# A condition vector fetched through the GpSimd queue, and the first two projections copied whole

## The chip, the cores and the metric

The kernel runs on one core of one Trainium2 chip. A core has five engines that run their own instruction streams side by side: TensorE (PE, matmuls and transposes into PSUM), ScalarE (ACT), VectorE (DVE), GpSimd (POOL) and SyncE (SP, which here only issues DMAs). They meet at semaphores. DMAs are issued by SP, and a few by ACT; sixteen DMA engines carry them out. The metric is the time of one execution in microseconds on the device, as the median over runs.

## The reference

A transformer block with adaptive layer norm, on one sequence of 2048 rows of 512 values (bf16):

```
mod = (silu(c) @ w_mod).reshape(1, 6, 1, 512)      # sa, ca, ga, sb, cb, gb
h = layernorm(x) * (1 + ca) + sa
q = (h @ wq)                                        # 32 heads of 128
k, v = last 512 rows of the caches                  # 8 groups, 4 heads each
o = softmax(q @ k.T / sqrt(128)) @ v
x = x + ga * (o @ wo)
h = layernorm(x) * (1 + cb) + sb
x = x + gb * (relu(h @ w1) @ w2)                    # inner width 1792
```

c is one row of 512 values; w_mod is 512 x 3072.

## The kernel before, in words

The rows are cut into 4 blocks of 512 (QB), and each block into 4 tiles of 128 rows. A unit is one block and one head: 128 units. For a unit, PE makes the projection of the head (4 matmuls of 512 columns, transposed so that the head's 128 values lie on the partitions), the scores against 512 keys (4 matmuls of 512 columns, in two pairs), and the product with the values (16 matmuls of 129 columns). ACT copies each projection from PSUM into a tile qT (L1485) and takes the exponential of each pair of scores (L1493); DVE divides by the row sums (L1503, L1504). The projection of a unit is made two units ahead (QA = 2), so the projections of units 0 and 1 are made before the main loop (L1689) starts. Output projections and, at the end, the two MLP layers fill PE as well.

A small scheduler, KB, keeps one list of operations for each engine in program order. Each operation names the resources that it reads and writes (`R_...`), and the scheduler turns them into semaphore waits. So the order of the Python lines is the order on each engine, and an operation that waits holds up everything behind it on its engine. `dma(..., eng=...)` puts a DMA into the stream of the engine named, SP if none is.

The change lies in the part before the main loop. That part goes as follows.

- Loads (L1559 to L1567). SP issues the first half of block 0's x, then c (as 4 rows of 128, into c_row), then the first half of the weights for the first two modulation vectors (`load_wm01(0)`, rows 0 to 255 of w_mod), then wq for heads 2 and 3, k and v of group 0. ACT issues the other half of x, the other half of those modulation weights, and wq for heads 0 and 1.
- POOL (L1568 to L1576) fills constants: ones, the exponent -0.5, the identity (affine select), epsilon, -1, the ones column beside v, and the constants added to the modulation columns.
- PE (L1578 to L1580) runs 7 warm-up matmuls on ones, transposes c (`silu_exp`, L1416), and runs 9 more warm-ups. ACT takes exp(-c) and a copy of c from PSUM, POOL makes silu from them (`silu_mul`, L1421 to L1423).
- Layer norm of block 0: DVE takes the statistics of tiles 0 to 2 (L1382, L1383), ACT those of tile 3 (L1582 to L1585), POOL raises to the power -0.5 (L1591), DVE normalises tiles 0 to 2 (L1393), POOL tile 3 (L1604).
- PE transposes tile 0 (L1375), makes the eight modulation columns of the first two vectors with 32 matmuls of one column each into bank 4 (`mod_cols_mm`; row chunks 0 and 1 of w_mod come from the first half of the weights, 2 and 3 from the second), and transposes tiles 1 to 3. DVE adds the constants (L1438).
- The transposed tiles get scale and shift in halves of 256 columns, on DVE (L1630) and ACT (L1632). `TB` names the banks in which the transposes stand: one row for each half, one entry for each chunk of 128 values.
- Then the projections of units 0 and 1 in halves of 256 columns. The first half of unit 0 goes to bank 4 (QBK), that of unit 1 to bank 5, the second half of unit 0 to bank 6, that of unit 1 to bank 4. ACT copies the two first halves (L1613), DVE the two second halves (L1611). A resource R_q1 stands for the second halves, and the scores of units 0 and 1 wait for both (L1492).

Of the kernel before, what the change touches and what calls it, by code (L numbers as in the profile page):

```python
# [8 lines left out]
ACTF = mybir.ActivationFunctionType  # L9
# [1189 lines left out]
def build_fast(nc, es, top, A_x, A_k_cache, A_v_cache, A_wq, A_wo, B_x, B_w1, B_w2, c, w_mod, out, flag):  # L1199
    P = 128  # L1200
# [24 lines left out]
    NQT = 3  # L1225
    VW = P + 8

    def T(name, shape, dt=BF):
        return es.enter_context(nc.sbuf_tensor(name, shape, dt))
# [6 lines left out]
    kT_sb = T("kT", [P, G, W])  # L1236
# [3 lines left out]
    qT = [T(f"qT{i}", [P, QB]) for i in range(NQT)]  # L1240
# [16 lines left out]
    c_row = T("c_row", [DC, P])  # L1257
# [10 lines left out]
    pr = [gaf[:, :], prv[:, 0:D], prv[:, D:2 * D], gbf[:, :]]  # L1268
# [9 lines left out]
    s_ps = [es.enter_context(nc.psum_tensor(f"psS{i}", [P, 2, 512], F32)) for i in range(2)]  # L1278
# [3 lines left out]
    bank = [s_ps[0][:, 0, :], s_ps[0][:, 1, :], s_ps[1][:, 0, :], s_ps[1][:, 1, :], q_ps[:, :],  # L1282
            o_ps[:, 0:2, :].rearrange("p a b -> p (a b)"), o_ps[:, 2:4, :].rearrange("p a b -> p (a b)"), w_ps[:, :]]
    QBK, WBK = 4, 7

    sem = lambda name: top.enter_context(nc.semaphore(name))
    kb = KB(nc)
    PE = kb.stream("pe", sem("s_pe"))
    ACT = kb.stream("act", sem("s_act"))
    DVE = kb.stream("dve", sem("s_dve"))  # L1290
    POOL = kb.stream("pool", sem("s_pool"))
    SP = kb.stream("sp", sem("s_sp"))

    def dsem(key):
        if key not in kb.dma_cnt:
            kb.add_dma_sem(key, sem("d_" + key))
        return key

    def dma(out_ap, in_ap, key, reads=(), writes=(), transpose=False, eng=None):
        k = dsem(key)  # L1300
        if transpose:
            return kb.op(SP, lambda e: e.dma_start_transpose(out_ap, in_ap), reads=reads, writes=writes, dma_sem=k)
        return kb.op(eng or SP, lambda e: e.dma_start(out_ap, in_ap), reads=reads, writes=writes, dma_sem=k)  # L1303

    RL = lambda name, n: [Res(f"{name}{i}") for i in range(n)]
    R_x, R_wq, R_wo = RL("x", NT), RL("wq", H), RL("wo", NPASS)
    R_kT, R_v, R_v1 = RL("kT", G), RL("v", G), Res("v1")
    R_hT, R_h2T = [RL(f"hT{i}_", DC) for i in range(2)], [RL(f"h2T{i}_", DC) for i in range(2)]
    R_qT, R_PT, R_o, R_oT = RL("qT", NQT), [RL(f"PT{i}_", 2) for i in range(NPT)], RL("o", NOS), RL("oT", NOT)
# [3 lines left out]
    R_b = RL("bank", 8)  # L1313
    R_ident, R_ones, R_c, R_sc, R_scf, R_tmp, R_cst = (Res(n) for n in ("ident", "ones", "c", "sc", "scf", "tmp", "cst"))
# [1 line left out]
    R_pr = [R_ga] + RL("pr", 2) + [R_gb]  # L1316
    R_st, R_mv, R_rstd = RL("st", NT), RL("mv", NT), RL("rstd", NT)
    R_h0 = RL("h0", DC)
    R_q1 = RL("q1_", 2)
    R_cf, R_m01 = Res("cf"), Res("m01")  # L1320
    R_s3, R_eps = Res("s3"), Res("eps")
    R_rinv, R_vmax, R_chk, R_good, R_flag = Res("rinv"), Res("vmax"), Res("chk"), Res("good"), Res("flag")
# [13 lines left out]
    def load_wq(h0, n, eng=None):  # L1336
        dma(wq_sb[:, :, h0 * Dh:(h0 + n) * Dh], wqv[:, :, h0 * Dh:(h0 + n) * Dh], f"wq{h0}", writes=R_wq[h0:h0 + n], eng=eng)
# [12 lines left out]
    def load_wm01(i, eng=None):  # L1350
        c0, c1 = i * DC // 2, (i + 1) * DC // 2
        dma(wm01[:, c0:c1, :], wm01v[:, c0:c1, :], f"wm{i}", writes=[R_wm[i]], eng=eng)

    def wm_res(sl, cc):
        return R_wm[cc // (DC // 2)] if sl < 2 else R_wm[sl]
# [15 lines left out]
    def mm(out_ap, lhsT, rhs, start, stop, reads, bk, signal):  # L1371
        kb.op(PE, lambda e: e.matmul(out_ap, lhsT, rhs, start=start, stop=stop), reads=reads, group_writes=[R_b[k] for k in bk], signal=signal)  # L1372
# [32 lines left out]
    def ln_tposes(tl, bks):  # L1405
        for cc in range(DC):
            bk = bks[cc]
            o = (cc % 2) * 512 + tl * P
            tpose(bank[bk].bitcast(BF)[:, o:o + P], xn[:, tl, cc * P:(cc + 1) * P], [R_xn[tl]], [bk], cc == DC - 1)

    CC_ORDER = (0, 2, 1, 3)
    QA = 2
# [12 lines left out]
    def mod_cols_mm(which, bk):  # L1425
        fs = []
        for cc in range(DC):
            for sl in (0, 1):
                for c2 in range(DC):
                    last = sl == 1 and c2 == DC - 1 and cc == DC - 1  # L1430
                    fs.append(lambda sl=sl, c2=c2, cc=cc, col=sl * DC + c2, last=last: mm(
                        bank[bk][:, col:col + 1], wm[sl][:, cc, c2 * P:(c2 + 1) * P], sc_bf[:, cc:cc + 1],
                        cc == 0 and sl == 0 and c2 == 0, last, [R_sc, wm_res(sl, cc)], [bk], last))
        return fs
# [49 lines left out]
    def q_evac(u, bk=QBK):  # L1484
        kb.op(ACT, lambda e: e.activation(qT[u % NQT][:, :], bank[bk], ACTF.Copy), reads=[R_b[bk]], writes=[R_qT[u % NQT]])  # L1485

    def s_mms(u, pr):
        b, h = units[u]
        g = h // R
        for i in range(2):  # L1490
            kc = pr * 2 + i
            mm(s_ps[pr][:, i, :], kT_sb[:, g, kc * P:(kc + 1) * P], qT[u % NQT][:, :], True, True, [R_kT[g], R_qT[u % NQT]] + ([R_q1[u]] if u < QA else []), [kc], i == 1)  # L1492
        kb.op(ACT, lambda e: e.activation(PT[u % NPT][:, pr * 2:pr * 2 + 2, :], s_ps[pr][:, :, :], ACTF.Exp, scale=scale),  # L1493
              reads=[R_b[pr * 2], R_b[pr * 2 + 1]], writes=[R_PT[u % NPT][pr]])

# [62 lines left out]

    for i in range(2):  # L1559
        dma(x_sb[:, 2 * i:2 * i + 2, :], xv[:, 2 * i:2 * i + 2, :], f"xa{i}", writes=R_x[2 * i:2 * i + 2], eng=ACT if i else SP)  # L1560
    dma(c_row[:, :], c[0].rearrange("(c p) -> c p", p=P), "c", writes=[R_c])
    load_wm01(0)
    load_wm01(1, ACT)
    load_wq(0, 2, ACT)
# [4 lines left out]
    kb.op(POOL, lambda e: e.memset(cst[:, 0:1], -0.5), writes=[R_cst])  # L1569
    kb.op(POOL, lambda e: e.affine_select(ident[:, :], ones[:, :], pattern=[[1, P]], compare_op=ALU.is_equal, fill=0.0,  # L1570
                                          base=0, channel_multiplier=-1), reads=[R_ones], writes=[R_ident])
    kb.op(POOL, lambda e: e.memset(cst[:, 1:2], eps), writes=[R_eps])
    kb.op(POOL, lambda e: e.memset(cst[:, 3:4], -1.0), writes=[R_eps])
    kb.op(POOL, lambda e: e.memset(v_sb[:, :, :, P:VW], 1.0), writes=[R_v1])
# [15 lines left out]
    def rstd_pow(lo, hi):  # L1590
# [12 lines left out]
    ln_norm(1)  # L1603
    kb.op(POOL, lambda e: e.tensor_scalar(xn[:, t3, :], x_sb[:, t3, :], s3[:, 1:2], rstd[:, t3:t3 + 1], op0=ALU.add, op1=ALU.mult),  # L1604
          reads=[R_x[t3], R_rstd[t3], R_s3], writes=[R_xn[t3]])
    TB = [[0, 0, 2, 2], [1, 1, 3, 7]]
    def q_evac_half(u, hf, bk, eng):
        src, dst = bank[bk][:, hf * HB:(hf + 1) * HB], qT[u][:, hf * HB:(hf + 1) * HB]
        w = [R_q1[u]] if hf else [R_qT[u]]
        if eng is DVE:  # L1610
            kb.op(DVE, lambda e: e.tensor_copy(dst, src), reads=[R_b[bk]], writes=w)  # L1611
        else:
            kb.op(ACT, lambda e: e.activation(dst, src, ACTF.Copy), reads=[R_b[bk]], writes=w)  # L1613

    ln_tposes(0, TB[0])
    fs = mod_cols_mm(0, QBK)
    for f in fs:
        f()
    ln_norm(2)
    mod_cols_evac(0, QBK)  # L1620
    HB = QB // 2
    R_half = [R_h0, R_hT[0]]

    def mod_half(hf, cc, eng):
        bk = TB[hf][cc]
        o = (cc % 2) * 512 + hf * HB
        src, dst = bank[bk].bitcast(BF)[:, o:o + HB], hT[0][:, cc, hf * HB:(hf + 1) * HB]
        sc, sh = modc[:, DC + cc:DC + cc + 1], modc[:, cc:cc + 1]
        if eng is DVE:
            kb.op(DVE, lambda e: e.tensor_scalar(dst, src, sc, sh, op0=ALU.mult, op1=ALU.add), reads=[R_b[bk], R_moda], writes=[R_half[hf][cc]])  # L1630
        else:
            kb.op(ACT, lambda e: e.activation(dst, src, ACTF.Identity, bias=sh, scale=sc), reads=[R_b[bk], R_moda], writes=[R_half[hf][cc]])  # L1632

    def q_half(u, hf, order, bk):
        for cc in order:
            mm(bank[bk][:, hf * HB:(hf + 1) * HB], wq_sb[:, cc, u * Dh:(u + 1) * Dh], hT[0][:, cc, hf * HB:(hf + 1) * HB], cc == CC_ORDER[0], cc == CC_ORDER[-1],
               [R_wq[u], R_half[hf][cc]], [bk], cc == CC_ORDER[-1])

    for tl in range(1, TPB):
        ln_tposes(tl, TB[tl // 2])  # L1640
    mod_half(0, 0, DVE)
# [5 lines left out]
    mod_half(1, 2, ACT)  # L1647
    mod_half(1, 1, DVE)
    mod_half(1, 3, DVE)
    q_evac_half(0, 0, QBK, ACT)  # L1650
    q_half(1, 0, CC_ORDER, 5)
    q_evac_half(1, 0, 5, ACT)
    q_half(0, 1, CC_ORDER, 6)
    q_evac_half(0, 1, 6, DVE)
    q_half(1, 1, CC_ORDER, QBK)
    q_evac_half(1, 1, QBK, DVE)
    load_wq(R, R)
    load_k(1)
    load_v(1)
# [5 lines left out]
    for g in range(G):  # L1665
        for i, op in enumerate((ALU.max, ALU.min)):
            add((3, 5, 12, 16, 20, 24, 28, 32)[g], lambda g=g, i=i, op=op: kb.op(DVE, lambda e: e.tensor_reduce(vmax[:, i, g:g + 1], v_sb[:, g, :, 0:Dh], axis=AX.XY, op=op),
                                                             reads=[R_v[g]], writes=[R_vmax]))
# [20 lines left out]
    for s in range(NU):  # L1689
        run_tasks(s, 100)  # L1690
        if wo_ready and wo_ready[0][0] <= s:
            _, b_, j_ = wo_ready.popleft()
            enqueue_wo(b_, j_)
        s_mms(s, 0)
        if s + QA < NU:
            q_mms(s + QA)
        s_mms(s, 1)
        if s >= 1:
            pv_mms(s - 1)
        pop_bg(4)  # L1700
# [100 lines left out]
def bass_adaLN_cond__sliding_block_cached__dense_activation_relu__prompt_kernel(  # L1801
# [14 lines left out]
    with ExitStack() as top:  # L1816
        flag = top.enter_context(nc.sbuf_tensor("flag", [1, 8], mybir.dt.int32))
        with ExitStack() as es:
            kb, fast, cut, dma_cnt, flag_ev = build_fast(nc, es, top, *args, flag)
            sems = dict(kb.sems)  # L1820
            meet = top.enter_context(nc.semaphore("s_meet"))
# [71 lines left out]
```

## Time and profile before

| | us |
|---|---|
| median of 3 runs | 560.51 |
| the runs | 561.1, 560.51, 560.2 |
| profiled execution, its own time | 561.1 |
| its span | 559.4 |
| PE busy | 550.5 (98%) |
| ACT busy | 348.9 (62%) |
| DVE busy | 253.8 (45%) |
| POOL busy | 54.7 (10%) |

The span runs from the first to the last instruction of the profile; the run's own time is 1.7 us longer. A row of the profile names the kernel's line, the engine, the operation, what it writes and reads by the program's names, and how often; bank names are psS (banks 0 to 3), psQ (4), psO (5 and 6) and psW (7). Where a helper issues the instruction the line is that of the helper: L1372 is every matmul, L1303 every plain DMA. The letter q behind an engine (SPq) marks its queue of issued instructions, PEld the loading of weights into PE. The text in square brackets is the idle time before an instruction and what ended it. DMA traffic is heaviest at the start: in the first tenth of the span the engines move about 225 GB/s, over the whole span 76.

### The profile page before, as it was taken

The page shows a single profiled execution, that of the slowest core. Times are in us where ns is not written, and L with a number is a line of the kernel's source. Part 1 is how long each engine was busy: PE and PEld are TensorE (multiplying, and loading weights), DVE is VectorE, ACT ScalarE, POOL GpSimd, SP SyncE. Part 2 cuts the span into 40 slices and gives each one's busy share as a digit, 9 for nine tenths or more (in the row PEclk, how much of TensorE's full clock was granted, in tenths as well). Part 3 has the DMA queues.
Part 4 walks back from the last instruction along what each step waited for, and adds up shares of the span by engine and source line. Part 5 has one row for each costly group of instructions (what it writes and reads, how often), then busy time and mean ns, then how long its engine had stood idle before and what let it go on. Part 6 is the DMA issues. An engine that isn't in the chain of part 4 may idle for free.

```text
span 559.4 us, 9666 instructions
## 1 busy us (share of the span) xinstructions
PE 550.5 (98%) x4060; PEld 315.8 (56%) x4134; DVE 253.8 (45%) x551; ACT 348.9 (62%) x453; POOL 54.7 (10%) x53
## 2 busy tenths in 40 slices
PE   8999999999999999999999999999999999999998
PEld 4665555555555555555555555555555654444444
DVE  4455555553546544335445443333354448321134
ACT  4986666666666666666666666666666644432500
POOL 3000022004410000033000000332000000000000
DMA  9897763513114144352352412111215110210001
GB/s 268 248 207 174 143 169 46 114 39 76 40 38 76 39 73 117 58 133 57 94 95 57 76 40 39 39 39 38 39 39 76 39 30 0 44 34 23 22 29 47
DMA packets 113309, 42.67 MB, mean 76 GB/s; under 512 B 93928, under 2 KB 112104, under 8 KB 113256
## 3 DMA queue, kind: packets, MB, share of 16 engines
q1 hardware_dynamic: 112024, 40.82, 34.3%
q10 hardware_dynamic: 1232, 1.15, 0.6%
q8 instruction: 33, 0.54, 0.4%
q14 instruction: 20, 0.16, 0.1%
HBM read 18.35 MB, written 2.10 MB: 37 GB/s over the span
## 4 chain that ended last, share of the span: by engine, by line
PE 98%; issue 1%; DMA 1%; DVE 0%; SPq 0%; DVEq 0%
PE psS L1372 28%; PE psO L1372 27%; PE psQ L1372 23%; PE psW L1372 20%; DMA c_row<-in_c_dram 1%; DVE qT L1611 0%; DVE hT L1630 0%; SPq L1303 0%; DVE PT L1723 0%; DVE PT L1725 0%; PE psS L1375 0%; PE psO L1416 0%; DVE modc L1438 0%; DVEq L123 0%
## 5 line engine op out<-in xcount | busy, mean ns | idle before, releaser
L1493 ACT ACTIVATE PT<-psS 128x1024 bf16<-128x1024 f32 x256 | 262.7, 1028 | 128.2 <-PE psS L1372 128.1
L1372 PE MATMUL psS<-qT,kT 128*128 128x512 bf16 x508 | 150.9, 379 | 0.5 <-DVE qT L1611 0.4
L1372 PEld LDWEIGHTS psO<-v,PT 128*128 128x128 bf16 x2048 | 126.6, 98 | 30.2
L1372 PE MATMUL psO<-v,PT 128*128 128x129 bf16 x2048 | 137.0, 220 | 0.0
L1372 PE MATMUL psQ<-hT,wq 128*128 128x512 bf16 (+1 forms) x510 | 130.5, 377 | 0.3 <-DVE hT L1630 0.2
L1503 DVE RECIPROCAL rinv<-psO 128x4 f32<-128x4 f32 x128 | 23.3, 182 | 227.2 <-PE psO L1372 227.2
L1372 PE MATMUL psW<-wo,oT 128*128 128x512 bf16 x454 | 118.1, 379 | 3.0
L1504 DVE TENSOR_TENSOR o<-psO,rinv 128x512 bf16<-128x512 f32 x128 | 88.5, 691 | 4.9 <-DVE rinv L1503 0.5
L1372 PEld LDWEIGHTS psQ<-hT,wq 128*128 128x128 bf16 x512 | 49.9, 98 | 60.3 <-issue 0.6
L1372 PEld LDWEIGHTS psS<-qT,kT 128*128 128x128 bf16 x512 | 49.5, 98 | 58.9 <-ACT PT L1493 0.7
L1485 ACT ACTIVATE qT<-psQ 128x512 bf16<-128x512 f32 x126 | 74.7, 593 | 0.0
L1712 ACT ACTIVATE wq<-psS 128x512 bf16<-128x512 f32 x56 | 33.4, 597 | 49.3 <-PE psS L1372 48.9
L1372 PEld LDWEIGHTS psW<-wo,oT 128*128 128x128 bf16 x512 | 45.0, 98 | 32.9 <-DVE acc L1526 1.2
L1526 DVE TENSOR_TENSOR acc<-psW,acc 128x512 f32<-128x512 f32 x48 | 33.2, 691 | 6.5 <-PE psW L1372 6.5
L1372 PE MATMUL psO<-wmw,wq 128*128 128x512 bf16 (+1 forms) x165 | 32.8, 352 | 0.3
L1529 POOL TENSOR_TENSOR acc<-acc,gaf 128x512 f32<-128x512 f32 x12 | 15.6, 1303 | 146.7 <-DVE acc L1526 139.8
L1388 POOL TENSOR_TENSOR rstd<-rstd,cst 128x4 f32<-128x4 f32 x7 | 7.2, 1025 | 216.8 <-DVE rstd L1387 216.8
L1723 DVE TENSOR_TENSOR PT<-psO,gbf 128x512 f32<-128x512 f32 (+1 forms) x12 | 7.5, 624 | 40.4 <-PE psO L1372 40.4
L1372 PE MATMUL psS<-h2T,wmw 128*128 128x512 bf16 x109 | 25.0, 379 | 0.2
L1372 PEld LDWEIGHTS psO<-wmw,wq 128*128 128x128 bf16 x168 | 15.3, 98 | 16.5
L1372 PE MATMUL psS<-hT,wmw 128*128 128x512 bf16 x110 | 24.4, 379 | 0.1
L1382 DVE BATCH_NORM_STATS2 st<-x 128x6 f32<-128x512 bf16 x31 | 21.1, 681 | 4.8 <-DMA x<-in_A_x_dram 4.8
(85 smaller groups left out, 192.6 us busy)
## 6 DMA issues: line engine op xcount, KB each, us to landing
wo<-in_A_wo_dram SPq DMA_DIRECT2D x4, 1024.0 KB, 5.9
wq<-in_A_wq_dram SPq DMA_DIRECT2D x7, 512.0 KB, 4.6
wmw<-in_B_w_dram SPq DMA_DIRECT2D x14, 256.0 KB, 3.1
wmw<-in_w_mod_dram SPq DMA_DIRECT2D x5, 512.0 KB, 4.8
oT<-o SPq DMA_TRANSPOSE x128, 2.4
out_dram<-PT SPq DMA_DIRECT2D x15, 128.0 KB, 1.7
x<-in_A_x_dram SPq DMA_DIRECT2D x3, 512.0 KB, 4.3
v<-in_A_v_cache_dram SPq DMA_DIRECT2D x8, 128.0 KB, 3.8
```

Of the source, the lines that this page charges most:

```text
L1372: kb.op(PE, lambda e: e.matmul(out_ap, lhsT, rhs, start=start, stop=stop), reads=reads, group_writes=[R_b[k] for k in bk], signal=signal)
L1382: kb.op(DVE, lambda e: e.bn_stats(st[:, t, :], x_sb[:, t, :]), reads=[R_x[t]], writes=[R_st[t]])
L1388: kb.op(POOL, lambda e: e.tensor_tensor(rstd[:, sl], rstd[:, sl], cst[:, 0:1].to_broadcast([P, hi - lo]), op=ALU.pow), reads=R_rstd[sl] + ...
L1485: kb.op(ACT, lambda e: e.activation(qT[u % NQT][:, :], bank[bk], ACTF.Copy), reads=[R_b[bk]], writes=[R_qT[u % NQT]])
L1493: kb.op(ACT, lambda e: e.activation(PT[u % NPT][:, pr * 2:pr * 2 + 2, :], s_ps[pr][:, :, :], ACTF.Exp, scale=scale), reads=[R_b[pr * 2], R ...
L1503: kb.op(DVE, lambda e: e.reciprocal(rinv[:, u, :], o_ps[:, :, P]), reads=[R_b[5], R_b[6]], writes=[R_rinv])
L1504: kb.op(DVE, lambda e: e.tensor_tensor(o_sb[u % NOS][:, :, :], o_ps[:, :, 0:P], rinv[:, u, :].unsqueeze(2).to_broadcast([P, TPB, P]), op=A ...
L1526: kb.op(DVE, lambda e: e.tensor_tensor(acc[:, tl, :], bank[WBK], acc[:, tl, :], op=ALU.add), reads=[R_b[WBK], R_acc[tl]], writes=[R_acc[tl]])
L1529: kb.op(eng, lambda e: e.tensor_tensor(acc[:, tl, :], acc[:, tl, :], gaf[:, :], op=ALU.mult), reads=[R_acc[tl], R_ga], writes=[R_acc[tl]])
L1712: kb.op(ACT, lambda e: e.activation(h1T[b % 2][:, fc, :], bank[bk], ACTF.Relu), reads=[R_b[bk]], writes=[R_h1[b % 2][fc]], pre=all_events( ...
L1723: kb.op(DVE, lambda e: e.tensor_tensor(yt[i][:, c0:c1], bank[bk][:, c0:c1], gbf[:, c0:c1], op=ALU.mult), reads=[R_b[bk], R_gb], writes=[R_ ...
```

## The change

The fetch of c leaves SP's queue, where it stood second, and is issued by GpSimd behind the affine select that makes the identity. On SP the first half of the modulation weights is then second. Half of the 32 modulation column matmuls run ahead of the transposes of tile 0. The copies in halves are gone: units 0 and 1 keep one bank each (4 and 5) for both halves of the projection, and each leaves with one ACT copy of 512 columns (`q_evac`, L1485), so that R_q1 is no longer needed. The last chunk of the second half is transposed into bank 6 in place of 7.

```diff
@@ s_mms
-            mm(s_ps[pr][:, i, :], kT_sb[:, g, kc * P:(kc + 1) * P], qT[u % NQT][:, :], True, True, [R_kT[g], R_qT[u % NQT]] + ([R_q1[u]] if u < QA else []), [kc], i == 1)
+            mm(s_ps[pr][:, i, :], kT_sb[:, g, kc * P:(kc + 1) * P], qT[u % NQT][:, :], True, True, [R_kT[g], R_qT[u % NQT]], [kc], i == 1)
@@ loads
-    dma(c_row[:, :], c[0].rearrange("(c p) -> c p", p=P), "c", writes=[R_c])
     load_wm01(0)
     load_wm01(1, ACT)
...
     kb.op(POOL, lambda e: e.affine_select(ident[:, :], ones[:, :], pattern=[[1, P]], compare_op=ALU.is_equal, fill=0.0,
                                           base=0, channel_multiplier=-1), reads=[R_ones], writes=[R_ident])
+    dma(c_row[:, :], c[0].rearrange("(c p) -> c p", p=P), "c", writes=[R_c], eng=POOL)
     kb.op(POOL, lambda e: e.memset(cst[:, 1:2], eps), writes=[R_eps])
@@ transposes and modulation columns
-    TB = [[0, 0, 2, 2], [1, 1, 3, 7]]
-    def q_evac_half(u, hf, bk, eng):
...
+    TB = [[0, 0, 2, 2], [1, 1, 3, 6]]
+    fs = mod_cols_mm(0, QBK)
+    for f in fs[:len(fs) // 2]:
+        f()
     ln_tposes(0, TB[0])
-    fs = mod_cols_mm(0, QBK)
-    for f in fs:
+    for f in fs[len(fs) // 2:]:
         f()
@@ projections of units 0 and 1
-    q_evac_half(0, 0, QBK, ACT)
     q_half(1, 0, CC_ORDER, 5)
-    q_evac_half(1, 0, 5, ACT)
-    q_half(0, 1, CC_ORDER, 6)
-    q_evac_half(0, 1, 6, DVE)
-    q_half(1, 1, CC_ORDER, QBK)
-    q_evac_half(1, 1, QBK, DVE)
+    for u, bk in ((0, QBK), (1, 5)):
+        q_half(u, 1, CC_ORDER, bk)
+        q_evac(u, bk)
```

More of the change, by code (lines that the diff above doesn't have):

```diff
@@ L1318, in build_fast @@
     R_h0 = RL("h0", DC)
-    R_q1 = RL("q1_", 2)
     R_cf, R_m01 = Res("cf"), Res("m01")
@@ L1605, in build_fast @@
           reads=[R_x[t3], R_rstd[t3], R_s3], writes=[R_xn[t3]])
-    TB = [[0, 0, 2, 2], [1, 1, 3, 7]]
-    def q_evac_half(u, hf, bk, eng):
[L1608 to L1613, printed above, removed]
+    TB = [[0, 0, 2, 2], [1, 1, 3, 6]]
+    fs = mod_cols_mm(0, QBK)
+    for f in fs[:len(fs) // 2]:
+        f()
     ln_tposes(0, TB[0])
-    fs = mod_cols_mm(0, QBK)
-    for f in fs:
+    for f in fs[len(fs) // 2:]:
         f()
```

## The prediction

> **What bounds the kernel now.** I read the page first (busy shares, then the chain that ended last), then the chain in order of time for the first 18 us, then the timeline of those microseconds by engine. The page says that TensorE (PE) is busy 98% of the span and that it carries the chain:
>
> ```profile
> PE 98%; issue 1%; DMA 1%; DVE 0%; SPq 0%; DVEq 0%
> ```
>
> So a microsecond saved or lost ahead of the first score matmul moves everything behind it by about as much; after 13.6 us PE shows no idle time worth naming. The edits lie wholly ahead of that point, where the chain in order of time is not compute (columns: start us, us, what):
>
> ```profile
> 0.79 0.40 SPq L1303
> 1.19 0.06 issue
> 1.24 3.66 DMA c_row<-in_c_dram
> ...
> 4.95 0.18 PE psO L1416
> 5.13 3.86 PE psW L1372 x9
> 8.98 0.22 PE psS L1375 x4
> 9.21 0.79 PE psQ L1372 x32
> ...
> 12.55 0.44 DVE qT L1611
> 12.99 0.35 issue
> 13.34 0.38 PE psS L1372
> ```
>
> The reader should see that the fetch of c, 1 KB, sets the start of everything: it is issued at 1.24, lands at 4.90, its transpose runs, and the nine warm-up matmuls queued behind that transpose hold PE until 8.82. At the other end stand the copies of the first projections out of PSUM. From the timeline (start, us, engine, line):
>
> ```profile
> 1.32 0.29 POOL L1570 TENSOR_SCALAR_AFFINE_SELECT ident<-ones 128x128 bf16<-128x128 bf16 x1 [0.30 <-POOL cst L1569]
> 1.66 0.41 SPq L1303 DMA_DIRECT2D wmw<-in_w_mod_dram  x1
> 4.95 0.18 PE L1416 MATMUL psO<-ident,c_row 4*128 4x4 bf16 x1 [0.73 <-DMA c_row<-in_c_dram]
> 5.43 0.28 POOL L1421 TENSOR_SCALAR tmp<-tmp 128x4 f32<-128x4 f32 x1 [3.17 <-ACT c_f L1418]
> 5.80 1.04 POOL L1422 TENSOR_TENSOR tmp<-tmp,cst 128x4 f32<-128x4 f32 x1
> 7.82 1.22 DVE L1393 TENSOR_SCALAR xn<-x,mv,rstd 128x512 bf16<-128x512 bf16 x3
> 8.82 0.39 PE L1375 MATMUL psS<-ident,xn 128*128 128x128 bf16 x4
> 12.55 0.43 DVE L1611 CAST qT<-psO 128x256 bf16<-128x256 f32 x1 [0.57 <-PE psO L1372]
> ```
>
> GpSimd (POOL) is free from 2.27 to 5.43, and PE stood idle 0.73 us for c.
>
> **The change part by part.**
>
> *c moves to POOL's queue.* Its issue goes behind the affine select, which ends at 1.61; on SP it was issued at 1.24, so 0.37 is given away at once. No row shows a DMA issued by POOL, so the time from issue to landing is bounded. From below: the quickest plain transfer in the view of DMA issues, 32 KB of the output at the quiet end, takes 1.5 us from issue to landing; 1.61 + 1.5 = 3.1. From above: c keeps the 3.66 it needed on SP, and software on POOL adds one small POOL operation, for which I take the 1.04 of the power on four columns (L1422): 1.61 + 1.04 + 3.66 = 6.3. Further off lies, in the same view, the 7.3 of the wq load on ACT's queue, which stood behind two large loads: 8.9. My value is near the middle of the first two: 1.61 + 1.04 + 1.5 = 4.15 quiet, plus 0.45 for other traffic (the excess of c on SP over a quiet transfer is 3.66 - 1.5 = 2.16; I take a fifth, since on a queue of its own c no longer stands behind the 256 KB of x, which land at 4.79, a tenth of a microsecond before c). That gives 4.6, **0.3 earlier** than 4.90; the ends give 1.8 earlier and 1.4 later.
>
> A later c is passed on in full. Queued behind the transpose on PE are the nine warm-ups (3.86); behind the two ACT copies of c are the statistics of tile 3 (L1582 to L1585); on POOL the silu and, behind it, the two powers for rstd, for which DVE's L1393 and then PE's transposes wait. An earlier c is passed on until x takes over: DVE's statistics start when x lands at 4.79 and its last small step ends at 7.69, so L1393 can start no earlier than 7.70 in place of 7.82.
>
> The memsets that POOL now issues after the transfer (L1572 to L1576, to 2.27 now) end some 1.04 later, at 3.3; the first reader is POOL's own L1421 at 5.43, so 2.1 us of cover hide them.
>
> [...]
>
> *SP's queue moves up.* w_mod's first half, wq for heads 2 and 3, k and v of group 0 and every later SP load are issued 0.42 earlier (1.66 - 1.24). The first half landed 6.3 after issue, at 7.9, and was first read at 9.0: 1.1 us of cover, so on the present path this is worth nothing. wq and k land by 9.8 and are read at 13.1. It would matter only if PE got to the modulation columns before 7.9.
>
> *Half of the 32 column matmuls go ahead of tile 0's transposes.* 0.79 and 0.22 lie in a row on PE now and then; the sum is the same while the normalised tile is ready (L1393's first third ends at 8.23) before the warm-ups end. Nothing, unless c is so early that PE waits for the tile. The bank of one transposed chunk (7 to 6) changes no order.
>
> *The first two projections leave in whole copies by ACT.* Now DVE copies the second half of unit 0 in 0.43 from 12.55, and the scores' weight load starts at 13.10. After, ACT copies all 512 columns from 12.55; this row has the time:
>
> ```profile
> L1485 ACT ACTIVATE qT<-psQ 128x512 bf16<-128x512 f32 x126 | 74.7, 593 | 0.0
> ```
>
> 0.59 - 0.43 = **+0.17** on the path. The two early ACT half copies (0.38 each, 11.68 to 12.50) ran beside PE and save nothing. Unit 1's copy follows on ACT until 13.73; the first exponential, now at 13.76, would be due at 13.93, so 0.2 us hide it. Bounds: 0 (ACT starts earlier than DVE did) and 0.6 (unit 1's copy in the way).
>
> **The sum** against the profiled execution: -0.3 + 0.17 = -0.1 on its 561.1 (span 559.4 and 1.7 around it). That run lies 0.6 above the median of the three, so on the median, 560.5, I forecast **560.4 us**. Its own range: c between 4.2 and 5.8, 559.9 to 561.6.
>
> **The rivals.**
>
> *Slower: GpSimd's transfer lands late.* One mechanism: descriptors made by software behind other POOL work, or a first use with a cost of its own, in a stage where the DMA engines are full from 2 us on. For it: 0.37 is lost at the start, no row shows such a transfer, and even on SP a 1 KB transfer took 3.66. Against: POOL is idle for three microseconds there. It decides from c at about 5.8 (+0.9 + 0.17 = +1.1). At 6.3 it gives 1.4 + 0.17 = +1.6, 562.1; at 8.9 it gives 4.0 + 0.17 = +4.2, 564.7.
>
> *Faster: c is early enough to close PE's gap.* If it lands by 4.2, PE never idles and x's statistics set the pace: transposes of tile 0 at 8.16 (L1393 from 7.70, 0.41 for a tile, 0.05) in place of 8.82, then 0.22 and the second half of the columns, 0.4, to 8.8; DVE's third L1393 runs to 9.04, and modc follows at 9.06 in place of 10.02. That is -0.96 + 0.17 = -0.8, 559.7. This is where the reordered columns and the earlier w_mod pay, since the first half needs w_mod by 7.7. To pass 0.2% it must bring 0.3 more, for which the warm-ups are a source: they start 0.43 apart, while later 512-column matmuls of the projections start 0.22 apart, so PE changes rate near 8.8. Without the gap the change could come earlier.
>
> *It moves nothing:* c lands at 4.9 as before, since the DMA engines are shared, and the copies cost their 0.17: 560.7.
>
> [...]
>
> **How the numbers follow.** Of a change of this kernel, 0.2%, 1.1 us, is about what a measurement can tell; the three runs spread over 0.9. Chances: forecast 0.40; it moves nothing 0.05 (both within 0.2%); slower rival 0.38; faster rival 0.17, of which 0.14 for going past 559.4. So faster 0.14, within 0.2% 0.40 + 0.05 + 0.03 = 0.48, slower 0.38. Both signs have weight, so the range is wider than the forecast's own: below to 559.3 (the faster rival with some rate gain), above to 562.8, which takes in c at 6.3 (562.1) and a later one by 0.7, and leaves the far end out.
>
> **What would show it.** In the new trace: the DMA issue on POOL near 1.6 and the c transpose on PE (L1416 now) at about 4.65, with PE's idle time before it near 0.4 us. If that transpose stands after 5.85 the slower rival holds, before 4.25 the faster one. Tile 0's transposes should follow it by some 3.9 us plus the first 16 columns; if they come later than that, w_mod's first half was late. The first whole ACT copy should take 0.59 and the first score matmul should start about 0.1 earlier than 13.34 in all. A first exponential further than 0.45 behind that matmul would show unit 1's copy in the way. The prediction is wrong as a whole if time after 14 us changes: it assumes the rest is only shifted.

## The result, and the profile after

The changed kernel takes 564.66 us (median of 6 runs, 564.01 to 564.86) against 560.55 before (6 runs, 560.2 to 561.1): ratio 1.007, 95% interval 1.0057 to 1.0083, 4.1 us slower. It lies outside the predicted range, which ended at 562.8, and on the side of the slower rival. The profiled execution took 564.17, its span is 562.4.

The chain of the changed kernel in order of time, first 18 us (start us, us, what):

```profile
1.33 0.26 POOL ident L1568
1.59 6.41 DMA c_row<-in_c_dram
8.00 0.05 issue
8.05 0.17 PE psO L1415
8.22 3.73 PE psW L1371 x9
...
12.99 0.18 DVE modc L1437
...
15.52 0.61 ACT qT L1484
16.13 0.35 issue
16.48 0.38 PE psS L1371
```

Everything hangs on c as before, but c lands at 8.00 in place of 4.90, 6.41 us after its issue. The later stations keep their distances: from the landing of c to modc 5.12 us before, 4.99 now; from modc to the first recorded score matmul 3.32 before, 3.49 now. So 3.10 - 0.13 + 0.17 = 3.14, and the score matmul moved from 13.34 to 16.48; the span grew by 3.0. The timeline shows what waited:

```profile
1.59 0.85 POOL L1303 DMA_DIRECT2D c_row<-in_c_dram  x1
4.90 0.69 DVE L1381 BATCH_NORM_STATS2 st<-x 128x6 f32<-128x512 bf16 x1 [4.90 <-DMA x<-in_A_x_dram]
8.05 0.17 PE L1415 MATMUL psO<-ident,c_row 4*128 4x4 bf16 x1 [3.82 <-DMA c_row<-in_c_dram]
8.53 0.28 POOL L1420 TENSOR_SCALAR tmp<-tmp 128x4 f32<-128x4 f32 x1 [5.36 <-ACT c_f L1417]
10.92 1.22 DVE L1392 TENSOR_SCALAR xn<-x,mv,rstd 128x512 bf16<-128x512 bf16 x3 [3.11 <-POOL rstd L1590]
```

x landed 0.1 us later than before and DVE's statistics of it were done at 7.8, but DVE waited 3.11 us for POOL, which stood behind the silu, and PE idled 3.82. The queues of the stretch from 2.44, where POOL's instruction ends, to 5.75, and of the stretch from there to 7.5 (kind: packets, MB, share of the DMA engines):

```profile
q1 hardware_dynamic: 335, 0.64, 54.8%
q10 hardware_dynamic: 258, 0.50, 41.3%
```

```profile
q10 hardware_dynamic: 366, 0.38, 64.0%
q1 hardware_dynamic: 379, 0.24, 43.8%
q0 software_dynamic: 32, 0.00, 1.2%
```

POOL's own queue, q0, moves nothing for 3.3 us after its instruction has ended; its 32 packets then stand among those of the other two queues. Busy time by stretch (us; length, PE, PEld, DVE, ACT, POOL, with the number of instructions in brackets, granted clock, DMA share, GB/s):

```profile
4.20:8.00 3.80, 0.02 (x1) 0.00 (x0) 2.73 (x8) 0.00 (x0) 0.00 (x0) 1.00 1.05 351
8.00:10.00 2.00, 1.95 (x6) 0.79 (x7) 0.00 (x0) 1.68 (x7) 1.33 (x2) 0.57 1.31 200
```

PE is empty until c lands, and then shows a granted clock of 0.57. The nine warm-ups take about as long as in the profiled execution of before (3.73 against 3.86), so between these two that costs nothing.

The medians differ by 4.1, the two profiled executions by 3.1. The profiled execution of before was the slowest of its six runs (561.1, 0.55 over the median), the one of after lies 0.5 under its median.

### The profile page after: what moved, and what is told of

It is laid out like the page before. It is cut to its first block, busy times and chain, and to the rows that moved or that the text cites. A ratio compares the mean times of both kernels' runs of the same rounds, so it can differ in the third digit from the quotient of the medians.

```text
span 562.4 us, 9664 instructions
## 1 busy us (share of the span) xinstructions
PE 550.3 (98%) x4060; PEld 315.8 (56%) x4134; DVE 253.0 (45%) x549; ACT 349.3 (62%) x453; POOL 55.7 (10%) x54
## 4 chain that ended last, share of the span: by engine, by line
PE 97%; DMA 1%; issue 1%; DVE 0%; ACT 0%; POOL 0%; POOLq 0%; DVEq 0%
PE psS L1371 28%; PE psO L1371 26%; PE psQ L1371 23%; PE psW L1371 20%; DMA c_row<-in_c_dram 1%; ACT qT L1484 0%; DVE hT L1623 0%; DVE PT L1713 0%; DVE PT L1715 0%; POOL ident L1568 0%; PE psS L1374 0%; POOL ones L1566 0%; DVE modc L1437 0%; PE psO L1415 0%; POOL cst L1567 0%
```

## The experiments

Times are medians, beside the kernel before on the same chip (560.3 to 560.4 in these comparisons), with the ratio and its 95% interval where several executions were timed.

**c alone on POOL** (half copies, banks and column order of before)

```diff
-    dma(c_row[:, :], c[0].rearrange("(c p) -> c p", p=P), "c", writes=[R_c])
...
+    dma(c_row[:, :], c[0].rearrange("(c p) -> c p", p=P), "c", writes=[R_c], eng=POOL)
     kb.op(POOL, lambda e: e.memset(cst[:, 1:2], eps), writes=[R_eps])
```

> The kernel before with one edit: c is issued by GpSimd behind the affine select; half copies, banks and column order stay. Theory (the late landing of c is the whole loss but for 0.17): c lands between 7.5 and 8.5 and the time is 564.0 to 564.7, some 3.5 to 4.1 above before. Rival (the whole copies or the reordered columns cost what the late c does not explain): below 563.5.

564.21 (1.0067, 1.0051 to 1.0084). Its chain:

```profile
1.59 6.54 DMA c_row<-in_c_dram
```

c landed at 8.1. This one line carries 3.8 of the 4.1 us.

**The rest alone**: c back on SP, whole copies, halved columns.

```diff
+    dma(c_row[:, :], c[0].rearrange("(c p) -> c p", p=P), "c", writes=[R_c])
     load_wm01(0)
...
-    dma(c_row[:, :], c[0].rearrange("(c p) -> c p", p=P), "c", writes=[R_c], eng=POOL)
```

> The changed kernel with c back as SyncE's second issue; whole copies by ScalarE, one bank each, half of the columns ahead of the transposes stay. Theory: c lands at 4.9 again, the copies cost their 0.17, so 560.5 to 561.1. Rival (the rest of the change costs more): 561.6 or more.

560.61 against 560.40 (1.0004, 0.9994 to 1.0014): no difference that can be told, and 0.2 is what the copies were to cost. c landed at 4.86:

```profile
1.24 3.62 DMA c_row<-in_c_dram
```

**Is a GpSimd transfer slow in itself?** The kernel before with fetches of c into tiles that nothing reads.

```diff
+    probe(POOL)
     kb.op(POOL, lambda e: e.memset(cst[:, 1:2], eps), writes=[R_eps])
...
+    def probes():
+        probe(POOL)
+        probe(SP)
...
+    for s_ in (10, 50, 75, 112):
+        add(s_, probes)
```

> The kernel before with extra fetches of c into scratch tiles that nothing reads: one by GpSimd behind the affine select, and a pair (GpSimd, then SyncE) at units 10, 50, 75 and 112. If a GpSimd transfer is slow in itself, all five take about 6 us from issue to landing. If it is the first use, the first takes about 6 and the later ones 2 to 3 also where the DMA engines are busy (unit 10). If it is the traffic, the first takes about 6, unit 10 something between, and the last ones 2 to 3, with the SyncE twins at 1.5 to 2.5. The output is that of the kernel before, the time within 1 us of it.

The probe at the change's place took 6.2 from issue to landing, although nobody waited for it. The next was issued at 9.50 (POOL's stream ran ahead to it) and took 3.6. The last three, issued at 159, 262 and 384, show in the view of DMA issues, one window each (KB, us to landing):

```profile
cprobe<-in_c_dram POOLq DMA_DIRECT2D x1, 1.0 KB, 2.1
```

```profile
cprobe<-in_c_dram POOLq DMA_DIRECT2D x1, 1.0 KB, 1.7
```

```profile
cprobe<-in_c_dram POOLq DMA_DIRECT2D x1, 1.0 KB, 1.8
```

SP's probes took 2.6 at 41 us, and 1.5 at 180, 268 and 397, as long as the quickest output on SP in the kernel before (32 KB, 1.5). So in quiet GpSimd took 0.2 to 0.6 longer than SP, and at the start some 4 us longer than in quiet. The run also shows an execution with c from SP that took 560.72, within the range of the kernel before on that chip (560.18 to 561.01). Its chain:

```profile
0.80 3.93 DMA x<-in_A_x_dram
4.73 0.02 issue
4.75 0.70 DVE st L1382
...
7.66 0.33 DVE xn L1393
7.99 0.05 issue
8.04 0.40 PE psS L1375 x4
```

c is not on it. PE's rate rose near 6.2, in the middle of the nine warm-ups, which took 2.83 in place of 3.92, and the transposes waited for the tile.

**First use or traffic?** The changed kernel with all loads but x held until c has landed.

```diff
+        dma(wm01[:, c0:c1, :], wm01v[:, c0:c1, :], f"wm{i}", reads=[R_c], writes=[R_wm[i]], eng=eng)
```

> The changed kernel, with every load but x and c held back until c has landed (the two loads of modulation weights wait for c, the others stand behind them on their queues). Theory of traffic (c's packets stand between those of x and the weights on all 16 engines): c lands 2 to 3.5 after issue, before 5. Theory of a first use (the first GpSimd transfer costs extra whatever the engines do): still 5.5 to 6.5 after issue, near 8. The time itself is worse in both cases, since the weights start late.

```profile
x<-in_A_x_dram SPq DMA_DIRECT2D x1, 256.0 KB, 4.0
x<-in_A_x_dram ACTq DMA_DIRECT2D x1, 256.0 KB, 4.2
c_row<-in_c_dram POOLq DMA_DIRECT2D x1, 1.0 KB, 3.6
```

3.6 in place of 6.4, with the same first use: c landed at 5.1, right behind x, a little above the 2 to 3.5 expected and far from the 5.5 to 6.5 of a first use. So it is the loads. The time, 564.8 in one execution, is that of late weights: the chain waits for wq until 13.1.

**An earlier place on POOL**: as the first operation, and ahead of the affine select.

```diff
+    dma(c_row[:, :], c[0].rearrange("(c p) -> c p", p=P), "c", writes=[R_c], eng=POOL)
     kb.op(POOL, lambda e: e.memset(ones[:, :], 1.0), writes=[R_ones])
```

> The changed kernel with c as GpSimd's very first operation, near 0.75, a microsecond before x's packets move; the warm-ups start 0.85 later. Theory of traffic: the descriptors are out before the engines are full, c lands at 2.5 to 4. Theory of a first use: 6 after issue, near 6.9.

> The changed kernel with c ahead of the affine select on GpSimd in place of behind it, some 0.4 earlier. Traffic: more than 0.4 earlier at landing, 6 to 7.5, and the time 562 to 564. First use: 0.4 earlier, 7.6, and about 564.2. If c could land before 4.5 here, 560.5.

Neither was issued ahead of the weights. As the first operation the transfer showed a start of only 1.31 and took 5.6, landing at 6.96, beside the two halves of the weights (7.0 and 7.5); ahead of the select it started at 1.37, took 6.4 and landed at 7.7. The first gave 562.41 in one execution, the second 564.76 (1.0075, 1.0058 to 1.0092). The expectations of traffic missed in both places (2.5 to 4, and 6 to 7.5 with 562 to 564), and the figures of a first use (6.9 and 7.6) came near. These two runs alone would not tell the theories apart, since neither issue came before that of the weights at 1.25; the run with the loads held does.

**Served in order of issue?** The changed kernel with the weights held only until POOL has issued c. The first version shared the resource of POOL's constants with the held loads, so that the next constant waited for the weights; the second mends that.

```diff
-    kb.op(POOL, lambda e: e.memset(cst[:, 1:2], eps), writes=[R_eps])
+    kb.op(POOL, lambda e: e.memset(cst[:, 1:2], eps), writes=[R_eps, R_go])
...
+        dma(wm01[:, c0:c1, :], wm01v[:, c0:c1, :], f"wm{i}", reads=[R_go], writes=[R_wm[i]], eng=eng)
```

> The changed kernel, with the loads of the modulation weights (and those behind them on their queues) held only until GpSimd has issued c, near 2.6, not until c has landed. Theory (c's packets are served behind what was issued before them, here x alone): c lands at 4.8 to 5.6, the weights about 1.3 later than now, near 8.5 to 9.2, and the time is 561 to 562. Rival (GpSimd's packets starve as long as the two other queues have work): c at 6.5 or later and the time 563.5 or more.

> The run with the weights behind c again, without the fault of that run: there GpSimd's second constant shared a resource with the held loads and waited for the weights to land, which put the silu some 4 us late whatever c did. Here only the loads wait for GpSimd's issue. Theory (served behind what was issued before): c lands at 5.2 to 5.6 as there; then the weights, near 10, hold the columns, and the time is 561.5 to 564. Rival (starved while the other queues have work): c at 6.5 or later and 564 or more.

c landed at 5.5 in the first version (568.16) and at 5.0 in the second:

```profile
wmw<-in_w_mod_dram SPq DMA_DIRECT2D x1, 512.0 KB, 7.8
wmw<-in_w_mod_dram ACTq DMA_DIRECT2D x1, 512.0 KB, 8.0
...
c_row<-in_c_dram POOLq DMA_DIRECT2D x1, 1.0 KB, 3.4
```

The two other queues had the weights issued to them from 2.6 on, and c did not starve: issued 1 us ahead of the weights, it took 3.4, issued 0.35 behind them, 6.4. The packets say the same. In the three runs with loads held, the first packet of POOL's queue went at 3.3 to 3.4, some 0.9 after POOL's instruction had ended and among the packets of x; in the other six with a GpSimd fetch at the start, between 5.7 and 5.9. So in these nine runs POOL's transfer waited some 2.4 longer for its first packet where the weights had been given to the two other queues before it. Its place behind them seems to be set where its instruction ends rather than where it begins: that of the first probe began 0.08 ahead of SP's half of the weights and ended 0.8 behind, and its first packet went at 5.8 as well, though ACT's half stood ahead of it in any case.

For c on SP the runs show no such wait. In the kernel before, ACT's half of the weights was issued 0.01 ahead of c and landed at 6.1, 1.2 behind it (the last row is from the view of DMA issues: KB, us to landing):

```profile
1.23 0.46 ACTq L1303 DMA_DIRECT2D wmw<-in_w_mod_dram  x1
1.24 0.36 SPq L1303 DMA_DIRECT2D c_row<-in_c_dram  x1
wmw<-in_w_mod_dram ACTq DMA_DIRECT2D x1, 512.0 KB, 4.9
```

The time of the second version, 565.02 (1.0081, 1.0064 to 1.0098), missed the expectation by a microsecond. The weights landed at 10.4 and 10.6, 3 us later than in the changed kernel for an issue 1.3 later; the chain has them in c's place:

```profile
2.59 7.84 DMA wmw<-in_w_mod_dram
10.43 0.14 issue
10.56 0.57 PE psQ L1371 x16
```

But the columns start at 10.56, in the changed kernel at 11.95. What was lost came behind them: to the first recorded score matmul it is 6.44 here and 4.53 there, with PE at half its rate. The same four projection matmuls in the two chains, here and in the changed kernel:

```profile
14.14 0.85 PE psO L1371 x4
```

```profile
14.61 0.44 PE psO L1371 x4
```

**PE's rate**: c alone on POOL, with 16 warm-ups in place of 7 ahead of c's transpose.

```diff
-    warm(7)
+    warm(16)
     silu_exp(5)
```

> The run with c alone on GpSimd, with 16 warm-up matmuls in place of 7 ahead of c's transpose, so that PE's idle time before it shrinks from some 3.9 to 2 us or less. Theory (part of the loss is PE's rate, which falls back while PE waits for the late c): the nine warm-ups behind the transpose run 0.22 apart, the transposes of tile 0 wait for the normalised tile, about 11.3 in place of 12.1, and the time falls by 0.5 to 1.0 below that run, to 563.2 to 563.7. Rival (the loss is c's landing alone, one to one): 564.0 to 564.5 as there.

563.63 (1.0059, 1.0045 to 1.0074), 0.58 below the run without. PE before the transposes of tile 0, without and with the added warm-ups:

```profile
8.17 0.18 PE L1416 MATMUL psO<-ident,c_row 4*128 4x4 bf16 x1 [3.95 <-DMA c_row<-in_c_dram]
8.28 3.96 PE L1372 MATMUL psW<-ones 128*128 128x512 bf16 x9
12.08 0.39 PE L1375 MATMUL psS<-ident,xn 128*128 128x128 bf16 x4
```

```profile
7.85 0.17 PE L1416 MATMUL psO<-ident,c_row 4*128 4x4 bf16 x1 [1.70 <-DMA c_row<-in_c_dram]
7.96 2.13 PE L1372 MATMUL psW<-ones 128*128 128x512 bf16 x9
11.19 0.40 PE L1375 MATMUL psS<-ident,xn 128*128 128x128 bf16 x4 [1.10 <-DVE xn L1393]
```

The nine ran at full rate, in 2.13 in place of 3.96, and then PE waited for the tile. The two profiled executions differ by 0.3 in c's landing as well, so not all of the 0.58 is rate for certain, and the times overlap (563.38 to 564.15 with the added warm-ups, 563.74 to 564.72 without). That the nine ran faster is shown; that the time fell is likely, not shown.

**An earlier c from ACT**: first on ACT ahead of x; first on ACT with both halves of x on SP; second on ACT behind x. All three have half of the columns ahead of the transposes and the half copies of before. The diff is that of the second; the first lacks the edit of x, and the third issues c behind that loop.

```diff
+    dma(c_row[:, :], c[0].rearrange("(c p) -> c p", p=P), "c", writes=[R_c], eng=ACT)
     for i in range(2):
-        dma(x_sb[:, 2 * i:2 * i + 2, :], xv[:, 2 * i:2 * i + 2, :], f"xa{i}", writes=R_x[2 * i:2 * i + 2], eng=ACT if i else SP)
+        dma(x_sb[:, 2 * i:2 * i + 2, :], xv[:, 2 * i:2 * i + 2, :], f"xa{i}", writes=R_x[2 * i:2 * i + 2])
```

> The kernel before with c issued by ScalarE ahead of its half of x, so that the first modulation weights are second on SyncE, and half of the columns ahead of tile 0's transposes; half copies kept. If c is what holds the start, c lands at 3 to 4, PE has no gap, and the statistics of x set the pace: 0.5 to 1.0 below before, 559.5 to 560.1. If something else (the first modulation weights, the statistics of tile 3 on ScalarE, which its later half of x delays by 0.4) takes its place at once: within 0.3 of before.

> The kernel before with both halves of x on SyncE and c first on ScalarE, ahead of its modulation weights, and half of the columns ahead of tile 0's transposes; half copies kept. In the run with c first on ScalarE the transfer behind c started late and the second half of x landed at 7.8. If that is due to the place behind the 1 KB transfer, x lands by 5 here, the second half of the weights takes the delay, and the time is 559.4 to 560.2. If the delay moves to whatever is needed next (the weights, later than 8.3), 560.4 to 562.

> The kernel before with c second on ScalarE, behind its half of x, in place of second on SyncE, and half of the columns ahead of tile 0's transposes; half copies kept. c should land at 4.5 to 4.9 as before; the two halves of the modulation weights change places (the first near 6.2, the second near 7.9), so the first columns no longer wait for the later half. If that wait counts: 559.9 to 560.2. If the normalised tile or the statistics hold PE anyway: within 0.2 of before.

None gains: 562.56 (1.0029, 1.0017 to 1.0042), 563.07 (1.0048, 1.0033 to 1.0063) and 562.89 (1.0035, 1.0023 to 1.0047). c landed at 2.1, 2.1 and 4.6, and each time what stood next in line came late. In the first it is ACT's half of x:

```profile
1.38 6.38 DMA x<-in_A_x_dram
7.76 0.02 issue
7.78 0.73 ACT xn L1582 x2
```

in the second the weights, landing at 8.4 and 8.6; in the third the second half of the weights:

```profile
1.84 8.39 DMA wmw<-in_w_mod_dram
10.23 0.05 issue
10.28 0.57 PE psQ L1372 x16
```

All three missed their expectations. The warm-ups were over by about 7, PE then idled (busy 0.60 of the 2 us from 8 to 10 in the first, 0.40 in the third), and in the profiled executions of these two its granted clock fell: it was 0.50 from 12 to 14. Most of the loss goes with that. Of the 18 executions the six with a mean granted clock of 1.0 took 560.85 to 561.6, the twelve at 0.994 to 0.997 took 562.4 to 564.3; without the fallen clock 0.45 to 1.2 us above before is left. The kernel before stays the fastest of all that were run.

## Why the prediction was wrong

- **c's landing** is the term that failed. The prediction took "0.45 for other traffic", "a fifth, since on a queue of its own c no longer stands behind the 256 KB of x", and arrived at 4.6; measured 8.0 (8.1, 7.8 and 7.7 in three other executions with a GpSimd fetch at that place). A queue of its own did not take c out of the line: behind the megabyte of weights issued on the two other queues at 1.24, 0.35 ahead of it, its fetch took 6.4, and with these held 3.4 to 3.9. The step had no row behind it. The nearest one, c on SP, even pointed the other way, since ACT's half of the weights, issued just ahead, had not held it. The quiet part was near, on the high side: 1.7 to 2.1 in all against 1.04 + 1.5. The traffic excess is 6.4 - 1.8 = 4.6, not 0.45.
- **The upper bound** was too low for the same reason: 6.3 carried over SP's wait behind x. The far end, 8.9, from a load that stood behind two large ones, was the comparable row, as the runs then showed, and the range left it out.
- **The slower rival** had the right place and sign, with a price given for c at 6.3 and at 8.9. Its one-to-one rule gives 3.1 + 0.17 = +3.3 for 8.0; measured +3.0 in the span of the profiled pair, +4.1 in the medians. Of its grounds a first use and POOL's own work fall away (with the same first use and the loads held c took 3.6, and POOL's instruction 0.85); what is left is the traffic issued ahead of c. That a later c is passed on in full held too: 3.10 at the landing became 3.14 at the score matmul.
- **The base** was one execution in which PE's rate rose only at the end of the nine warm-ups. The probe run shows one in which it rose near 6.2 and x's statistics set the pace. So part of the 0.6 by which the profiled execution lay above the median was probably lost there, and in an execution like that of the probe run c at 4.6 is hidden behind x. Two slips in the sums are small: c at 4.2 gives 560.0, not 559.9, and in the faster rival DVE's third L1393, started at 7.70, ends at 8.92, not 9.04. That a late c also costs rate was not in the sum; the run with more warm-ups puts it at up to about 0.6, within the spread of its executions.
- **The copies**: +0.17 predicted, +0.17 in the distance from modc to the score matmul. **The columns and the earlier w_mod** were costed at nothing. The run with c back on SP, which has the columns, shows nothing; w_mod's first half landed at 7.3 in place of 7.9, with no reader before 11.8. **The memsets** on POOL ended at 3.17 (3.3 predicted) and hid.

What is not settled: why POOL's transfer waits. The runs show only that it depends on what the other queues were given before it, and that most of it lies ahead of the first packet (in the changed kernel at 5.76, for an instruction that ended at 2.44; with the weights held at 3.3 to 3.4, among the packets of x). Where the last half microsecond of the changed kernel's median goes was not profiled either.

Nor do the runs settle what PE's rate follows. In the changed kernel the nine warm-ups ran at a granted clock of 0.57, behind 3.82 of idle PE. In the run with c alone PE idled 3.95, the granted clock in the view is 1.00 throughout, and yet the nine took 3.96: there the granted clock does not tell PE's rate.

## What to carry to other kernels

GpSimd's queue was no lane of its own: a small transfer that the start waits for landed there together with or behind the large ones that the other queues had been given first (c at 8.0, the weights at 7.3 and 7.8), and at 5.0 where these were issued 1 us behind it; so what counted was its place behind their issue. For SP and ACT between themselves this was not seen (c on SP at 4.90, ACT's half of the weights, issued 0.01 ahead of it, at 6.1). Price a moved transfer by a row with the same bytes ahead of it, not by its size. Before costing a start-up to a tenth of a microsecond, see whether the profiled execution stands near the median, and whether PE's rate rose early or late in it (here the nine warm-ups took 2.83 or 3.92).

## What was unexpected in the hardware

What was issued behind c, a 1 KB transfer, on ACT's queue landed later than in the kernel before: half a megabyte of weights took 8.4 us with c second there, and 256 KB of x took 6.4 with c first, where they took 4.9 and 4.2; in the changed kernel, with c on neither queue, the weights took 6.6. In the run with c second on ACT the DMA engines carried only 55 GB/s from 8 to 10 us, while those weights were still due. But the run with the weights behind c has a like stretch, 48 GB/s from 10 to 12 us while wq was due, with no 1 KB transfer on those queues. So the small transfer is not shown to be the cause.
